# A fused S5 state-space and SwiGLU kernel: the first token block chunk by chunk through three features, its first weights in pieces of two features, and the parameter work behind all roots

## The chip, the cores and the metric

The kernel runs on one core of a Trainium2 chip. A core has a matrix engine (TensorE, written PE in the profile, with its weight loads in a row of their own, PEld), a vector engine (VectorE, DVE), an engine for activation functions (ScalarE, ACT), a general engine (GpSimd, POOL) and a queue that mostly starts transfers (SyncE, SP). The metric is the device time of one execution in microseconds. The kernel before takes 212.93 us, the median of three executions (212.89, 212.93, 213.28).

## The reference

The input x has 2048 tokens of 512 values (bf16). Every token is normalised, and three terms are added:

```python
xn = _layernorm(x, axis=-1)
# A: a diagonal complex recurrence over the tokens
Lam_bar = exp(exp(log_dt) * Lambda)
B_bar = ((Lam_bar - 1) / Lambda)[:, None] * Bmat
h_t = Lam_bar * h_(t-1) + B_bar @ xn_t
A = 2 * real(h @ Cmat.T) + xn * Dskip
# B: a gated feed-forward layer, 512 -> 1792 -> 512
B = (silu(xn @ w1) * (xn @ w3)) @ w2
out = x + A + B
```

The state has 512 complex entries. `Lambda_re`, `Lambda_im` and `log_dt` are the "parameters" below: 512 numbers each, from which the columns and tables of the recurrence are made once, at the start.

## The kernel before, in words

The tokens are cut into four blocks of 512, each block into four chunks of 128. The 1792 features of the feed-forward layer are 14 tiles of 128, called features 0 to 13 here. For each block the kernel runs three stages: `glu_up` (gate and up projections, L358), `ssm_in` (the input projection of the recurrence, L388) and `y_out` (the down projection and the state's output, L461). The order of the stages is glu_up 0, ssm_in 0, ssm_in 1, glu_up 1, y_out 0, and so on to y_out 3.

The schedule is manual (L68): every engine executes its instructions in the order in which the program writes them, and the framework adds the waits. Work of VectorE that isn't urgent (statistics of later blocks, tables, the recurrence) stands in a queue of tasks, each with a cost in microseconds, and `drain` (L339) takes tasks from it at a given rate while the matmuls are written.

One matmul here has a stationary operand of 128x128 and streams up to 512 columns. For block 0 the stationary operands are pieces of w1 and w3 and the streamed columns are the normalised tokens, transposed (`xnT`), so `glu_mm` (L353) can process any stretch of tokens of a feature: four matmuls over the four parts of the inner dimension, for the columns `ts`.

What the change touches is the opening, before the first block runs at full width:

- L74 to L76: three small transfers of the parameters into `prm`, issued by ACT's queue. Then x of block 0, chunk by chunk, on SP's queue (L78, L79), then w1 and w3 by `load_w13` (L86): features 0 to 2, 3 to 5, x of block 1, features 6 to 9, 10 to 13.
- `keep_warm` (L133): matmuls of a zero tile into a bank that nobody reads. Five of 512 columns stand first (L138), three after the transpose of the parameters (L227, L228).
- `stats` (L146), `aggr` (L150), `rstd_act` (L153) and `normed` (L172): the normalisation of a chunk on DVE, ACT (Ln, then Exp) and DVE. `turn` (L231) transposes a normalised chunk on TensorE into PSUM, four transposes of 128x128, and `put` (L237) copies it into `xnT` on ACT or DVE.
- `par_cols` (L253): the parameters' columns, two activations on ACT and six small operations on POOL; `r_col` (L497) is an Exp of POOL's first product.
- L485 to L514: the order of all this. Parameter columns first; then chunks 0 and 1 up to `xnT`; then chunks 2 and 3 to `xn`, with a table load for Silu on ACT behind their roots (L503); then features 0 to 2 for the columns of chunks 0 and 1 (256 columns), with the transposes of chunks 2 and 3 put in ahead of the last group; then the two copies.

`glu_up(0, 1.3, begun)` (L524) takes the three begun features, adds the columns of chunks 2 and 3 and goes on with feature 3 at full width. [...]

Of the kernel before, what the change touches and what calls it, by code (L numbers as in the profile page):

```python
# [15 lines left out]
BF16 = DT.bfloat16  # L16
P = 128
# [3 lines left out]
def kernel(  # L21
# [24 lines left out]
    nc = tc.nc  # L46
# [3 lines left out]
    TBLK = 512  # L50
# [4 lines left out]
    NDT = D // P  # L55
    NPT = PS // P
# [7 lines left out]
    const = ctx.enter_context(tc.tile_pool(name="const", bufs=1))  # L64
    xpool = ctx.enter_context(tc.tile_pool(name="xpool", bufs=NBLK))
    work = ctx.enter_context(tc.tile_pool(name="work", bufs=2))
    psum = ctx.enter_context(tc.tile_pool(name="psum", bufs=8, space=bass.MemoryType.PSUM))
    ctx.enter_context(tc.manual_schedule())  # L68

    def ps_tile(name):  # L70
        return psum.tile([P, 512], FP32, name=name, tag="ps")


    prm = const.tile([3 * NPT, P], BF16, name="prm")  # L74
    for i, src in enumerate((A_Lambda_re, A_Lambda_im, A_log_dt)):
        nc.scalar.dma_start(out=prm[i * NPT:(i + 1) * NPT, :], in_=src.rearrange("(t p) -> t p", p=P))  # L76
    x_blk = [xpool.tile([P, CPB, D], BF16, name="x_blk") for _ in range(NBLK)]
    for c in range(CPB):  # L78
        nc.sync.dma_start(out=x_blk[0][:, c, :], in_=xv[:, 0, c, :])  # L79
    w1_sb = const.tile([P, NDT, F], BF16, name="w1_sb")  # L80
    w3_sb = const.tile([P, NDT, F], BF16, name="w3_sb")
    w2_sb = const.tile([P, NFT, D], BF16, name="w2_sb")
    w1v = B_w1.rearrange("(t p) f -> p t f", p=P)
    w3v = B_w3.rearrange("(t p) f -> p t f", p=P)

    def load_w13(f0, f1):  # L86
        fs = slice(f0 * P, f1 * P)
        nc.sync.dma_start(out=w1_sb[:, :, fs], in_=w1v[:, :, fs])
        nc.sync.dma_start(out=w3_sb[:, :, fs], in_=w3v[:, :, fs])

    dskip_row = const.tile([P, D], BF16, name="dskip_row")
# [3 lines left out]
    def load_turned(dst, src):  # L95
        for t in range(NDT):
            nc.sync.dma_start_transpose(out=dst[:, t, :], in_=src[:, t * P:(t + 1) * P])

    load_w13(0, 3)
    load_w13(3, 6)  # L100
    nc.sync.dma_start(out=x_blk[1], in_=xv[:, 1, :, :])
    load_w13(6, 10)
    load_w13(10, NFT)
    nc.sync.dma_start(out=dskip_row, in_=A_Dskip.partition_broadcast(P))
# [8 lines left out]
        load_turned(ct[1], A_C_im)  # L113


    warm = const.tile([P, 512], BF16, name="warm")
    nc.vector.memset(warm, 0.0)
    halfpi = const.tile([P, 1], FP32, name="halfpi")
    nc.vector.memset(halfpi, float(np.pi / 2))
# [2 lines left out]
    ident = const.tile([P, P], BF16, name="ident")  # L122
# [8 lines left out]
    wps = ps_tile("warm_ps")  # L131

    def keep_warm(n, width=512):  # L133
        for _ in range(n):
            nc.tensor.matmul(out=wps[:, :width], lhsT=warm[:, :P], rhs=warm[:, :width], start=True, stop=True)  # L135

    nc.scalar.preload_act_table_set("natural_log_exp_and_others")
    keep_warm(5)  # L138


    mv_all = const.tile([P, NBLK * CPB, 2], FP32, name="mv_all")
    rstd_all = const.tile([P, NBLK * CPB], FP32, name="rstd_all")
    xnTs = [None] * NBLK
    sums = {}

    def stats(c):  # L146
        sums[c] = work.tile([P, 6], FP32, name="stats", bufs=4)
        nc.vector.bn_stats(out=sums[c], in_=x_blk[c // CPB][:, c % CPB, :])  # L148

    def aggr(c):  # L150
        nc.vector.bn_aggr(out=mv_all[:, c, :], in_=sums.pop(c))

    def rstd_act(c0, c1):  # L153
        y = rstd_all[:, c0:c1]
        nc.scalar.activation(out=y, in_=mv_all[:, c0:c1, 1], func=ACT.Ln, bias=eps)
        nc.scalar.activation(out=y, in_=y, func=ACT.Exp, scale=-0.5)
# [15 lines left out]
    def normed(c):  # L172
        xn = work.tile([P, D], BF16, name="xn", bufs=8)
        nc.vector.tensor_scalar(out=xn, in0=x_blk[c // CPB][:, c % CPB, :], scalar1=mv_all[:, c, 0:1],
                                scalar2=rstd_all[:, c:c + 1], op0=ALU.subtract, op1=ALU.mult)
        return xn
# [47 lines left out]

    new_xnT(0)
    pprm = psum.tile([P, 3 * NPT], BF16, name="prm_ps", tag="ps")
    nc.tensor.transpose(out=pprm, in_=prm, identity=ident[:3 * NPT, :3 * NPT])  # L227
    keep_warm(3)  # L228
    xn0 = xns_of[0] = {}

    def turn(c):  # L231
        pxt = psum.tile([P, NDT, P], BF16, name="xt_ps", tag="ps")
        for dt in range(NDT):
            nc.tensor.transpose(out=pxt[:, dt, :], in_=xn0[c][:, dt * P:(dt + 1) * P], identity=ident)  # L234
        return pxt

    def put(c, pxt, eng):  # L237
        dst = xnTs[0][:, :, c * P:(c + 1) * P]
        if eng is nc.scalar:
            nc.scalar.activation(out=dst, in_=pxt, func=ACT.Copy)  # L240
        else:
            nc.vector.tensor_copy(out=dst, in_=pxt)  # L242
# [10 lines left out]
    def par_cols():  # L253
        prmc = const.tile([P, 3 * NPT], FP32, name="prmc")
        nc.scalar.activation(out=prmc, in_=pprm, func=ACT.Copy)
        col["lre"], col["lim"], col["ldt"] = (prmc[:, i * NPT:(i + 1) * NPT] for i in range(3))
        nc.scalar.activation(out=c4("dt"), in_=col["ldt"], func=ACT.Exp)
        nc.gpsimd.tensor_tensor(out=c4("kr"), in0=col["dt"], in1=col["lre"], op=ALU.mult)
        nc.gpsimd.tensor_tensor(out=c4("ki"), in0=col["dt"], in1=col["lim"], op=ALU.mult)
        nc.gpsimd.tensor_scalar(out=c4("turn"), in0=col["ki"], scalar1=float(1.0 / (2.0 * np.pi)), scalar2=None,  # L260
                                op0=ALU.mult)
        tt = nc.gpsimd.tensor_tensor
        tt(out=c4("den"), in0=col["lre"], in1=col["lre"], op=ALU.mult)
        tt(out=c4("d2"), in0=col["lim"], in1=col["lim"], op=ALU.mult)
        tt(out=col["den"], in0=col["den"], in1=col["d2"], op=ALU.add)
# [73 lines left out]
    def drain(us):  # L339
        credit[0] = min(credit[0] + us, us + 1.5)  # L340
        while queue and credit[0] > 0:
            cost, task = queue.popleft()
            credit[0] -= cost
            task()
# [8 lines left out]
    def glu_mm(b, f, w_sb, ps, ts):  # L353
        for dt in range(NDT):
            nc.tensor.matmul(out=ps[:, ts], lhsT=w_sb[:, dt, f * P:(f + 1) * P], rhs=xnTs[b][:, dt, ts],  # L355
                             start=(dt == 0), stop=(dt == NDT - 1))

    def glu_up(b, rate, begun=()):  # L358
        hg[b] = work.tile([P, NFT, TBLK], BF16, name="hgT")
        late = None  # L360
        for f in range(NFT):
            if f < len(begun):
                g_ps, u_ps = begun[f]
                ts = slice(TBLK // 2, TBLK)
            else:
                g_ps, u_ps = ps_tile("g_ps"), ps_tile("u_ps")
                ts = slice(0, TBLK)
            glu_mm(b, f, w1_sb, g_ps, ts)
            glu_mm(b, f, w3_sb, u_ps, ts)
            sl16 = work.tile([P, TBLK], BF16, name="sl16", bufs=4)  # L370
            nc.scalar.activation(out=sl16, in_=g_ps, func=ACT.Silu)  # L371
            up16 = work.tile([P, TBLK], BF16, name="up16", bufs=4)
            nc.scalar.activation(out=up16, in_=u_ps, func=ACT.Copy)  # L373
            if for_act:
                for_act.popleft()()
            if late is not None:
                late()

            def late(f=f, sl16=sl16, up16=up16):
                nc.vector.tensor_tensor(out=hg[b][:, f, :], in0=sl16, in1=up16, op=ALU.mult)  # L380

            drain(rate)
        late()
# [98 lines left out]
                nc.sync.dma_start(out=ov[:, c, ds], in_=o16[:, ds])  # L482


    AHEAD = 3  # L485
    par_cols()
    for c in range(2):
        stats(c)
        aggr(c)
        rstd_act(c, c + 1)  # L490
    xn0[0] = normed(0)
    xn0[1] = normed(1)
    put(0, turn(0), nc.scalar)
    keep_warm(2, P)
    put(1, turn(1), nc.scalar)
    keep_warm(4, 2 * P)
    nc.scalar.activation(out=r_col, in_=col["kr"], func=ACT.Exp)  # L497
    stats(2)
    stats(3)
    aggr(2)  # L500
    aggr(3)
    rstd_act(2, 4)
    nc.scalar.preload_act_table_set("silu_and_others")  # L503
    xn0[2] = normed(2)
    xn0[3] = normed(3)
    begun = []
    for f in range(AHEAD):
        begun.append((ps_tile("g_ps"), ps_tile("u_ps")))
        glu_mm(0, f, w1_sb, begun[f][0], slice(0, TBLK // 2))
        if f == AHEAD - 1:  # L510
            t2, t3 = turn(2), turn(3)
        glu_mm(0, f, w3_sb, begun[f][1], slice(0, TBLK // 2))
    put(2, t2, nc.scalar)
    put(3, t3, nc.vector)  # L514

    push([(3.2, par_turns), (0.2, par_recip)])
    push([(0.0, lambda: for_act.extend(par_trig()))])
# [4 lines left out]
    push([(1.2, par_out)])  # L522
    push(ln_tasks(2))
    glu_up(0, 1.3, begun)  # L524
    assert not for_act
    ssm_in(0, 0.8)
# [3 lines left out]
    push(res_tasks(2))  # L530
    push(res_tasks(3))
    glu_up(1, 1.35)
    y_out(0, 4.0)
    ssm_in(2, 0.85)
    glu_up(2, 1.35)
    y_out(1, 4.0)
    ssm_in(3, 0.85)
# [33 lines left out]
```

## Time and profile before

| what | value |
|---|---|
| median of three executions | 212.93 us (212.89 to 213.28) |
| the profiled execution | 213.02 us |
| its span, first to last instruction | 211.2 us |
| PE busy | 207.1 us, 98% of the span |
| DVE busy | 173.3 us, 82% |
| ACT busy | 94.0 us, 45% |
| POOL busy | 5.4 us, 3% |
| first useful matmul (L355) | starts at 7.12 us |
| feature 3 of block 0 (L355, 512 columns) | starts at 13.17 us |

The span is measured from the first instruction to the last; the execution's own time is 1.82 us longer. Times in the timeline are microseconds from the start of the span. A line of it gives the start, the duration, the engine, the line of the program, the operation, output and inputs by the program's names, the shape, and how many such instructions were merged into the line; in brackets stands how long the engine had been idle and what ended it. Matmuls overlap one another, so the distance between two starts says what one costs, and not the duration of one. PEclk, the clock that the throttle granted, is full in every slice.

### The profile page before, as it was taken

The page shows a single profiled execution, that of the slowest core. Times are in us where ns is not written, and L with a number is a line of the kernel's source. Part 1 is how long each engine was busy: PE and PEld are TensorE (multiplying, and loading weights), DVE is VectorE, ACT ScalarE, POOL GpSimd, SP SyncE. Part 2 cuts the span into 40 slices and gives each one's busy share as a digit, 9 for nine tenths or more (in the row PEclk, how much of TensorE's full clock was granted, in tenths as well). Part 3 has the DMA queues.
Part 4 walks back from the last instruction along what each step waited for, and adds up shares of the span by engine and source line. Part 5 has one row for each costly group of instructions (what it writes and reads, how often), then busy time and mean ns, then how long its engine had stood idle before and what let it go on. Part 6 is the DMA issues. An engine that isn't in the chain of part 4 may idle for free.

```text
span 211.2 us, 2809 instructions
## 1 busy us (share of the span) xinstructions
PE 207.1 (98%) x1005; PEld 97.3 (46%) x1005; DVE 173.3 (82%) x343; ACT 94.0 (45%) x164; POOL 5.4 (3%) x27
## 2 busy tenths in 40 slices
PE   7999999999999999999999999999999999999994
PEld 2764444444444444444444444444444444444453
DVE  4599899997999999999999999999999999121111
ACT  4689866666666300066666600036666630000000
POOL 4000230000000000000000000000000000000000
PEclk9999999999999999999999999999999999999999
DMA  5999589953000000000002100100000000000010
GB/s 151 342 348 199 93 191 327 221 124 75 0 0 3 0 25 25 25 26 3 0 0 67 33 3 25 50 25 0 5 0 0 0 0 26 28 25 25 33 44 26
DMA packets 26054, 13.69 MB, mean 65 GB/s; under 512 B 15928, under 2 KB 26040, under 8 KB 26040
## 3 DMA queue, kind: packets, MB, share of 16 engines
q1 hardware_dynamic: 26016, 13.51, 26.3%
q8 instruction: 8, 0.13, 0.3%
q14 instruction: 6, 0.05, 0.1%
q10 hardware_dynamic: 24, 0.00, 0.0%
HBM read 7.74 MB, written 2.10 MB: 47 GB/s over the span
## 4 chain that ended last, share of the span: by engine, by line
PE 97%; DMA 1%; ACTq 0%; DVE 0%; issue 0%
PE g_ps L355 23%; PE y_ps L471 23%; PE u_ps L355 23%; PE y_ps L476 13%; PE bu_ps L394 13%; PE warm_ps L135 1%; DMA prm<-in_A_log_dt_dram 1%; PE xt_ps L234 1%; ACTq L76 0%; DVE xnT L242 0%; DVE o L481 0%; PE prm_ps L227 0%
## 5 line engine op out<-in xcount | busy, mean ns | idle before, releaser
L355 PEld LDWEIGHTS <-w_sb 128*128 128x128 bf16 x472 | 46.0, 98 | 51.0 <-DVE xnT L242 0.4
L355 PE MATMUL g_ps<-xnT,w_sb 128*128 128x512 bf16 (+1 forms) x236 | 58.0, 368 | 0.1
L355 PE MATMUL u_ps<-xnT,w_sb 128*128 128x512 bf16 (+1 forms) x236 | 58.0, 368 | 0.0
L471 PE MATMUL y_ps<-w_sb,hgT 128*128 128x512 bf16 (+2 forms) x238 | 51.2, 366 | 0.0
L373 ACT ACTIVATE up<-u_ps 128x512 bf16<-128x512 f32 x56 | 33.5, 598 | 15.8 <-PE u_ps L355 15.3
L396 ACT ACTIVATE u<-bu_ps 128x512 bf16<-128x512 f32 x32 | 19.1, 597 | 46.3 <-PE bu_ps L394 46.3
L371 ACT ACTIVATE sl<-g_ps 128x512 bf16<-128x512 f32 x56 | 33.4, 597 | 10.6 <-PE g_ps L355 10.4
L428 DVE TENSOR_TENSOR_SCAN ab<-r_col,h,ab 128x256 bf16<-128x256 f32 x56 | 37.6, 731 | 0.2
L471 PEld LDWEIGHTS <-hgT 128*128 128x128 bf16 x238 | 22.8, 98 | 25.9
L481 DVE TENSOR_TENSOR o<-y_ps,x_blk 128x512 bf16<-128x512 f32 (+2 forms) x17 | 11.1, 653 | 24.3 <-PE y_ps L476 24.3
L476 PE MATMUL y_ps<-ct,h 128*128 128x512 bf16 (+2 forms) x136 | 30.4, 366 | 0.0
L394 PE MATMUL bu_ps<-xnT,bt 128*128 128x512 bf16 x128 | 28.1, 379 | 0.0
L380 DVE TENSOR_TENSOR hgT<-sl,up 128x512 bf16<-128x512 bf16 x56 | 23.0, 414 | 3.1 <-ACT up L373 3.1
L476 PEld LDWEIGHTS <-h 128*128 128x128 bf16 x136 | 13.0, 98 | 14.7
L394 PEld LDWEIGHTS <-bt 128*128 128x128 bf16 x128 | 12.5, 98 | 15.1
L148 DVE BATCH_NORM_STATS2 stats<-x_blk 128x6 f32<-128x512 bf16 x16 | 10.5, 675 | 1.7 <-DMA x_blk<-in_A_x_dram 1.7
L437 DVE TENSOR_TENSOR ab<-ab,tab_s 128x2048 bf16<-128x2048 bf16 x8 | 9.8, 1223 | 0.2
L433 DVE TENSOR_TENSOR ab<-ab,tab_c 128x2048 bf16<-128x2048 bf16 x8 | 9.8, 1221 | 0.1
L413 DVE TENSOR_TENSOR ab<-u,tab_y 128x2048 bf16<-128x2048 bf16 x8 | 9.7, 1218 | 0.0
L410 DVE TENSOR_TENSOR ab<-u,tab_x 128x2048 bf16<-128x2048 bf16 x8 | 9.7, 1217 | 0.0
L183 DVE TENSOR_TENSOR x_blk<-xd,x_blk 128x512 bf16<-128x512 bf16 x16 | 6.8, 428 | 0.5
L182 DVE TENSOR_TENSOR xd<-xn,dskip_row 128x512 bf16<-128x512 bf16 x16 | 6.7, 418 | 0.0
(72 smaller groups left out, 80.0 us busy)
## 6 DMA issues: line engine op xcount, KB each, us to landing
w_sb<-in_B_w_dram SPq DMA_DIRECT2D x4, 512.0 KB, 8.2
out_dram<-o SPq DMA_DIRECT2D x15, 128.0 KB, 1.7
w_sb<-in_B_w_dram SPq DMA_DIRECT2D x1, 1792.0 KB, 8.1
w_sb<-in_B_w_dram SPq DMA_DIRECT2D x4, 384.0 KB, 4.4
x_blk<-in_A_x_dram SPq DMA_DIRECT2D x3, 512.0 KB, 6.8
x_blk<-in_A_x_dram SPq DMA_DIRECT2D x4, 128.0 KB, 2.3
xnT<-xn SPq DMA_TRANSPOSE x12, 2.4
dskip_row<-in_A_Dskip_dram SPq DMA_DIRECT2D x1, 128.0 KB
```

The costliest lines, as they stand in the source:

```text
L148: nc.vector.bn_stats(out=sums[c], in_=x_blk[c // CPB][:, c % CPB, :])
L355: nc.tensor.matmul(out=ps[:, ts], lhsT=w_sb[:, dt, f * P:(f + 1) * P], rhs=xnTs[b][:, dt, ts], start=(dt == 0), stop=(dt == NDT - 1))
L371: nc.scalar.activation(out=sl16, in_=g_ps, func=ACT.Silu)
L373: nc.scalar.activation(out=up16, in_=u_ps, func=ACT.Copy)
L380: nc.vector.tensor_tensor(out=hg[b][:, f, :], in0=sl16, in1=up16, op=ALU.mult)
L394: nc.tensor.matmul(out=u_ps, lhsT=bt[ri][:, dt, pt * P:(pt + 1) * P], rhs=xnTs[b][:, dt, :], start=(dt == 0), stop=(dt == NDT - 1))
L396: nc.scalar.activation(out=u16[:, :, pt, ri, :], in_=u_ps.rearrange("p (s t) -> p s t", s=NSB), func=ACT.Copy)
L428: nc.vector.tensor_tensor_scan(out=a[:, pt, 2 * ri + 1, :], data0=r_b, data1=a[:, pt, 2 * ri, :], initial=init, op0=ALU.mult, op1=ALU.add)
L433: nc.vector.tensor_tensor(out=a[:, :, 0::2, :], in0=a[:, :, 1::2, :], in1=tab_b("c"), op=ALU.mult)
L471: nc.tensor.matmul(out=y_ps[:, ds], lhsT=hg[b][:, f, cl * P:(cl + 1) * P], rhs=w2_sb[:, f, ds], start=(f == 0), stop=False)
L476: nc.tensor.matmul(out=y_ps[:, ds], lhsT=h_tiles[i][:, pt, ri, h_ts], rhs=ct[ri][:, pt, ds], start=False, stop=(pt == NPT - 1 and ri == 1))
L481: nc.vector.tensor_tensor(out=o16[:, ds], in0=y_ps[:, ds], in1=x_blk[b][:, cl, ds], op=ALU.add)
```

## The change

It changes the order and the grain of the opening; nothing after feature 2 of block 0 is written differently.

- ACT's queue begins with the first table load, then issues w1 of features 0 and 1, and then the three parameter transfers. `load_w13` gets an argument for the queue of its first half. The weights of features 0 to 5 come in three pairs of pieces of two features, not two pairs of three.
- The warm-up tile is 128 columns wide instead of 512 and is read repeatedly by a broadcast; eight warm-ups of 512 columns stand first, four of 128 columns behind the transposes of chunk 0, and the others are gone.
- The transposes and copies of chunk 0 are cut into two halves with a PSUM tile each: ACT copies one, DVE the other. `turn` and `put` get a range.
- Every chunk has its own root (`rstd_act` of one column). Statistics, roots, normalisations and copies of neighbouring chunks are interleaved on DVE and ACT.
- Features 0 and 1 run chunk by chunk (128 columns) for chunks 0, 1 and 2, feature 2 for chunks 0 and 1 together (256 columns) and then chunk 2. `glu_up` adds chunk 3 alone.
- The transpose of the parameters, their columns, `r_col` and the table load for Silu come behind the fourth root. The copy of chunk 3 is on ACT behind them.

```diff
-    prm = const.tile([3 * NPT, P], BF16, name="prm")
-    for i, src in enumerate((A_Lambda_re, A_Lambda_im, A_log_dt)):
-        nc.scalar.dma_start(out=prm[i * NPT:(i + 1) * NPT, :], in_=src.rearrange("(t p) -> t p", p=P))
...
-    def load_w13(f0, f1):
+    def load_w13(f0, f1, first=nc.sync):
         fs = slice(f0 * P, f1 * P)
-        nc.sync.dma_start(out=w1_sb[:, :, fs], in_=w1v[:, :, fs])
+        first.dma_start(out=w1_sb[:, :, fs], in_=w1v[:, :, fs])
         nc.sync.dma_start(out=w3_sb[:, :, fs], in_=w3v[:, :, fs])
...
-    load_w13(0, 3)
-    load_w13(3, 6)
+    nc.scalar.preload_act_table_set("natural_log_exp_and_others")
+    load_w13(0, 2, nc.scalar)
+    prm = const.tile([3 * NPT, P], BF16, name="prm")
+    for i, src in enumerate((A_Lambda_re, A_Lambda_im, A_log_dt)):
+        nc.scalar.dma_start(out=prm[i * NPT:(i + 1) * NPT, :], in_=src.rearrange("(t p) -> t p", p=P))
+    load_w13(2, 4)
+    load_w13(4, 6)
...
-    warm = const.tile([P, 512], BF16, name="warm")
+    warm = const.tile([P, P], BF16, name="warm")
...
     def keep_warm(n, width=512):
+        rhs = warm.unsqueeze(1).to_broadcast([P, width // P, P])
         for _ in range(n):
-            nc.tensor.matmul(out=wps[:, :width], lhsT=warm[:, :P], rhs=warm[:, :width], start=True, stop=True)
-
-    nc.scalar.preload_act_table_set("natural_log_exp_and_others")
-    keep_warm(5)
+            nc.tensor.matmul(out=wps[:, :width], lhsT=warm, rhs=rhs, start=True, stop=True)
+
+    keep_warm(8)
...
     pprm = psum.tile([P, 3 * NPT], BF16, name="prm_ps", tag="ps")
-    nc.tensor.transpose(out=pprm, in_=prm, identity=ident[:3 * NPT, :3 * NPT])
-    keep_warm(3)
...
-                ts = slice(TBLK // 2, TBLK)
+                ts = slice(TBLK - P, TBLK)
...
-    AHEAD = 3
+    def new_xt(n=NDT):
+        return psum.tile([P, n, P], BF16, name="xt_ps", tag="ps")
+
+    def ahead(fs, w_sbs, c0, c1):
+        for f in fs:
+            for w_sb in w_sbs:
+                glu_mm(0, f, w_sb, begun[f][w_sb is w3_sb], slice(c0 * P, c1 * P))
+
+    H = NDT // 2
+    ta, tb, t1 = new_xt(H), new_xt(H), new_xt()
+    begun = [(ps_tile("g_ps"), ps_tile("u_ps")) for f in range(3)]
+
+    stats(0)
+    aggr(0)
+    rstd_act(0, 1)
+    stats(1)
+    xn0[0] = normed(0)
+    aggr(1)
+    rstd_act(1, 2)
+    turn(0, ta, 0, H)
+    turn(0, tb, H, NDT)
+    keep_warm(4, P)
+    put(0, ta, nc.scalar, 0, H)
+    stats(2)
+    put(0, tb, nc.vector, H, NDT)
+    xn0[1] = normed(1)
+    aggr(2)
+    rstd_act(2, 3)
+    stats(3)
+    ahead((0, 1), (w1_sb,), 0, 1)
+    turn(1, t1)
+    put(1, t1, nc.vector)
+    ahead((0, 1), (w3_sb,), 0, 1)
+    nc.tensor.transpose(out=pprm, in_=prm, identity=ident[:3 * NPT, :3 * NPT])
+    xn0[2] = normed(2)
+    aggr(3)
+    rstd_act(3, 4)
     par_cols()
-    for c in range(2):
-        stats(c)
-        aggr(c)
-        rstd_act(c, c + 1)
-    xn0[0] = normed(0)
-    xn0[1] = normed(1)
-    put(0, turn(0), nc.scalar)
-    keep_warm(2, P)
-    put(1, turn(1), nc.scalar)
-    keep_warm(4, 2 * P)
     nc.scalar.activation(out=r_col, in_=col["kr"], func=ACT.Exp)
-    stats(2)
-    stats(3)
-    aggr(2)
-    aggr(3)
-    rstd_act(2, 4)
     nc.scalar.preload_act_table_set("silu_and_others")
-    xn0[2] = normed(2)
     xn0[3] = normed(3)
-    begun = []
-    for f in range(AHEAD):
-        begun.append((ps_tile("g_ps"), ps_tile("u_ps")))
-        glu_mm(0, f, w1_sb, begun[f][0], slice(0, TBLK // 2))
-        if f == AHEAD - 1:
-            t2, t3 = turn(2), turn(3)
-        glu_mm(0, f, w3_sb, begun[f][1], slice(0, TBLK // 2))
-    put(2, t2, nc.scalar)
-    put(3, t3, nc.vector)
+    ahead((0, 1), (w1_sb, w3_sb), 1, 2)
+    ahead((2,), (w1_sb,), 0, 2)
+    t2, t3 = new_xt(), new_xt()
+    turn(2, t2)
+    put(2, t2, nc.vector)
+    ahead((2,), (w3_sb,), 0, 2)
+    ahead((0,), (w1_sb, w3_sb), 2, 3)
+    turn(3, t3)
+    put(3, t3, nc.scalar)
+    ahead((1, 2), (w1_sb, w3_sb), 2, 3)
```

More of the change, by code (lines that the diff above doesn't have):

```diff
@@ L226, with turn, put @@
     pprm = psum.tile([P, 3 * NPT], BF16, name="prm_ps", tag="ps")
-    nc.tensor.transpose(out=pprm, in_=prm, identity=ident[:3 * NPT, :3 * NPT])
-    keep_warm(3)
     xn0 = xns_of[0] = {}
[L231 to L238, printed above, removed]
+    def turn(c, pxt, d0=0, d1=NDT):
+        for dt in range(d0, d1):
+            nc.tensor.transpose(out=pxt[:, dt - d0, :], in_=xn0[c][:, dt * P:(dt + 1) * P], identity=ident)
+    def put(c, pxt, eng, d0=0, d1=NDT):
+        dst = xnTs[0][:, d0:d1, c * P:(c + 1) * P]
         if eng is nc.scalar:
```

## The prediction

> **What bounds the kernel now.** I read the page first: the busy shares and the chain that ended last.
>
> ```profile
> PE 207.1 (98%) x1005; PEld 97.3 (46%) x1005; DVE 173.3 (82%) x343; ACT 94.0 (45%) x164; POOL 5.4 (3%) x27
> PE 97%; DMA 1%; ACTq 0%; DVE 0%; issue 0%
> ```
>
> TensorE (PE) is busy for 98% of the span and is 97% of the chain. So only two things shorten the kernel: fewer matmul cycles, or useful matmuls that start earlier. The change takes no useful matmul away, so the opening decides. I read it in the timeline of the first 14 us (start, duration, instruction).
>
> ```profile
> 1.17 2.31 PE L135 MATMUL warm_ps<-warm 128*128 128x512 bf16 x5 [1.17 <-DVE eps L121]
> 2.79 0.69 DVE L148 BATCH_NORM_STATS2 stats<-x_blk 128x6 f32<-128x512 bf16 x1 [1.66 <-DMA x_blk<-in_A_x_dram]
> 3.51 0.18 DVE L151 BATCH_NORM_AGGREGATE mv_all<-stats 128x2 f32<-128x6 f32 x1
> 3.84 0.18 ACT L255 ACTIVATE prmc<-prm_ps 128x12 f32<-128x12 bf16 x1 [0.62 <-PE prm_ps L227]
> 4.05 0.21 ACT L257 ACTIVATE c_dt<-prmc 128x4 f32<-128x4 f32 x1
> 4.16 0.28 ACT L155 ACTIVATE rstd_all<-mv_all,eps 128x1 f32<-128x1 f32 x1
> 4.47 0.20 ACT L156 ACTIVATE rstd_all<-rstd_all 128x1 f32<-128x1 f32 x1
> 4.71 0.83 DVE L174 TENSOR_SCALAR xn<-x_blk,mv_all,rstd_all 128x512 bf16<-128x512 bf16 x2 [0.22 <-ACT rstd_all L156]
> 5.18 0.61 PE L234 MATMUL xt_ps<-ident,xn 128*128 128x128 bf16 x4
> 5.83 1.24 ACT L240 ACTIVATE xnT<-xt_ps 128x512 bf16<-128x512 bf16 x2 [0.73 <-PE xt_ps L234]
> 6.22 1.05 PE L135 MATMUL warm_ps<-warm 128*128 128x256 bf16 x4
> 7.12 0.60 PE L355 MATMUL g_ps<-xnT,w_sb 128*128 128x256 bf16 x4
> 7.65 0.61 PE L355 MATMUL u_ps<-xnT,w_sb 128*128 128x256 bf16 x4
> 9.41 0.61 PE L234 MATMUL xt_ps<-ident,xn 128*128 128x128 bf16 x8
> 9.85 0.60 PE L355 MATMUL u_ps<-xnT,w_sb 128*128 128x256 bf16 x4
> 10.54 0.61 PE L355 MATMUL g_ps<-xnT,w_sb 128*128 128x256 bf16 x4
> 13.17 1.03 PE L355 MATMUL g_ps<-xnT,w_sb 128*128 128x512 bf16 x4
> ```
>
> Four readings. The first useful matmul starts at 7.12, behind a chain: x lands, statistics, root, normalise, transpose, copy out. Feature 3, the first at full width, starts at 13.17 (call this T3); from there to 211.2 are 198.03 us that the change leaves alone. So the forecast is the shift of T3. Third, the four warm-up matmuls of 256 columns from 6.22 take until about 7.07, 213 ns each, while useful ones of 256 columns take 0.435 us for four, 109 ns: TensorE runs at half rate until about 6.95, some 5.8 us after its first matmul, although the granted clock is 1.00 throughout. Fourth, PE waits little after 7.12: 0.21 for weights before 7.65, 0.36 for a transposed chunk before 10.54.
>
> **The change, part by part.** The sum is made against the profiled execution: 213.02 us, span 211.2, so 1.82 around it. It lies 0.09 above the median of 212.93.
>
> Parameter work leaves the front. ACT's prmc and c_dt (3.84, 4.05) no longer precede the first Ln. The first aggregation ends at 3.69, so Ln starts at 3.74, Exp 0.31 later (4.16 to 4.47), normalisation 0.24 after that (4.47 to 4.71): 4.29. The second statistics, ahead of it on DVE, run 3.61 to 4.27, so 4.30, 0.41 earlier. Turning chunk 0 starts 0.47 later (4.71 to 5.18): 4.77. This needs ACT free at 3.74. The table load (1.28) goes first, from 0.71 to 1.99, then four issues: one of weights (SP's early ones take 0.43 to 0.51) and three of prm (0.56, 0.26, 0.31), to about 3.6 if nothing overlaps. Margin 0.1; if the queue runs beside the load, 1.4.
>
> Warm-ups. The three after the prm transpose, the two of 128 and the four of 256 columns go; they filled waits and cost nothing. DVE's memset of 512 columns takes 0.27; a quarter of it lets PE start at about 1.0. Eight matmuls at 0.43 run to 4.43. PE then idles 0.34 until 4.77; before, it idled 0.37 from 3.27 to 3.64.
>
> Chunk 0 is copied out in halves. At half rate two transposes are ready 0.44 after the start (four took 0.65, two cost 0.21): 5.21. ACT first does the second root (aggregation 4.63 to 4.81, Ln 4.86, Exp 5.17), so its half starts at 5.28. 256 columns take between 0.20 (the tiny ACT forms) and 0.60 (512 columns); I take 0.40: 5.68. DVE does the third statistics first (4.80 to 5.48), then its half, between 0.21 and 0.42, taken 0.27: 5.75. So one chunk is ready at 5.80 where two were ready at 7.07.
>
> Work of features 0 to 2. Before: 48 matmuls of 256 columns at 109 ns, 5.2 us. After: 8 of 256 and 80 of 128. The last 22 matmuls of the kernel are also 128 columns wide with new weights each; the chain of waits has them as
>
> ```profile
> 207.27 0.78 PE y_ps L471 x14
> 208.05 0.46 PE y_ps L476 x8
> ```
>
> that is 56 ns each. So 80 × 56 + 8 × 109 = 5.35 us: +0.13. [...] The trace here has 56.
>
> Now the order, with full rate from 6.95 as in the trace. Chunk 0 against w1, 8 matmuls at 107 ns: 5.80 to 6.65. Chunk 1 was normalised by DVE at about 5.75 to 6.15; its turn runs 6.65 to 7.02 and is copied out 7.25 to 7.67 (0.42), DVE having finished aggregation and statistics at 6.9. Chunk 0 against w3: to 7.46, then the prm transpose. Chunk 1, 16 matmuls: 7.72 to 8.60. Feature 2 w1, 4 of 256: 9.04. Turn 2: 9.26. Feature 2 w3: 9.70. Copy 2 is out at 9.95 (9.53 + 0.42), a wait of 0.3. Feature 0 chunk 2: 10.0 to 10.44; turn 3: 10.66; features 1 and 2 chunk 2: 11.54. Copy 3 on ACT is queued behind the parameter columns, the POOL product and the table load. The third and fourth normalisations follow at 7.6 and 8.68, the fourth root's Exp at 8.44, so prmc 8.55, c_dt 8.75, r_col 0.55 later (c_dt to POOL's product took 0.5): 9.3, table load 9.5 to 10.8, copy 3 10.9 to 11.5. It ends with the matmuls. Chunk 3, 24 matmuls: 11.55 to 12.87. T3 is 12.87: −0.30.
>
> If full rate comes by 5.8, chunk 1 goes out at 6.85 to 7.27 and everything follows 0.4 earlier: T3 = 12.47, −0.70. If it comes at 7.85: 13.07, −0.10. The four times shown (212.89, 212.93, 213.02 profiled, 213.28) are as they would be if the moment wanders a little. Eight full warm-ups fill 1.0 to 4.43 without the gap at 3.27, so I lean to the earlier half: −0.50.
>
> Weights. w1 of features 0 and 1 is 262 KB instead of 393, issued by ACT between 0.75 and 2.0 instead of SP's 2.64. Summing the half-microsecond rows of DMA rates, x and the first 393 KB (917 KB) were moved by 5.65; the new w1 is inside 786 KB, moved by about 5.3; the old piece was moved by 5.65 and landed at 6.24 (2.64 + 3.6), so the new one lands near 5.8, just in time, or earlier. w3, inside 1.05 MB: moved by 6.1, about 6.8 landed, needed at 7.0. SP gets one issue more (0.5) ahead of block 1's x and all later loads; those are used from 14.2 on, and the transposed B at 32: no cost. The three prm transfers, now behind w1 on ACT's queue, are issued by 3.6 and land 1.9 later (1.59 to 3.50 in the chain before): 5.5, and PE asks for them at 7.46: no cost unless they are 2 us late, when every later matmul would wait behind that transpose. POOL's c_turn ends near 10.0 and DVE's next work needs it only at 10.0 to 10.4, where it started at 10.39: nothing. ACT starts evacuating at 11.9 instead of 11.18 against an earlier T3; each feature takes it 1.2 to 1.85 and PE 1.73, and the banks of feature 0 are needed again at T3 + 1.73 = 14.6, freed at 13.1: nothing.
>
> **Rivals.** (a) The clock does not come. The new PE idles (0.34 at 4.43, some 0.15 at 5.63) restart whatever releases the full rate. 5.8 us after 4.77 is 10.6; until then chunk 0 w3 ends at 7.93, chunk 1 takes 1.70 (to 9.73), feature 2 w1 0.85 (10.58), and the rest at full rate gives T3 = 14.42: +1.25, 214.3. For it: a third of the opening is transposes and idling. Against: the 0.37 gap before did no such harm. Each microsecond of delay costs about 0.5, and it decides from about 8.1 on. [...]
>
> (b) Transfers collide. If ACT issues w1 at 0.75, its 262 KB share the engines with chunks x 1 to 3. Ahead of x 2 wholly it costs 262 KB at 263 GB/s (the row at 2.5 to 3.0), 1.0 us; not at all, 0. x 2 was due at 3.7 to 4.3 and its statistics, which stand ahead of the chunk 0 copy on DVE, need it at 4.80, so 0 to 0.5 late: T3 between 12.67 and 13.35, so 212.5 to 213.2.
>
> (c) Weight loads bind. If loads of 98 ns did not overlap, 80 × (98 − 56) = +3.4, 216. The tail speaks against it.
>
> (d) PE hardly waits at all: 5.80 + 5.35 + 16 transposes less 4 (0.67) gives 11.9: −1.2, 211.8.
>
> **How the numbers follow.** About 0.2% (0.43 us) is what a measurement can tell from no change. Forecast (0.56): −0.10 to −0.70, taken −0.50 from 212.93, 212.43; 0.40 of it beyond 0.43. (b) 0.18: 0.04 faster, 0.12 same, 0.02 slower. (a) 0.17, nearly all slower. (c) 0.02. (d) 0.07. Together faster 0.51, same 0.28, slower 0.21. The range reaches (a) at 214.3 and part of (d), 211.9; left out are (c), a later (a) and the best of (d), some 0.15. The forecast's own is 212.2 to 212.85.
>
> **What would show it.** First Ln at 3.74 and first normalisation at 4.30; first useful matmul near 5.8; 128-column matmuls 56 ns apart; the step from 107 to 56 ns by 7; waits of 0.3 or less before chunks 2 and 3; feature 3 at 12.5 to 12.9, and 198.0 us from there. I am wrong if the first statistics start after 2.8, if the table load ends after copy 3 is turned, or if 107 ns lasts past 8.

## The result, and the profile after

The changed kernel takes 214.50 us (median of 22 executions, 213.06 to 214.94); the kernel before, on the same chips, 213.08 (22 executions, 212.85 to 213.93). The ratio is 1.0053, with a 95% interval of 1.0038 to 1.0068 (the two medians alone would give 1.0067): slower, where a gain of 0.50 us was forecast. The times lie in two groups: 17 between 214.19 and 214.94, and 5 between 213.06 and 213.37. The profiled execution took 214.55, its span is 212.8; it belongs to the larger group.

The page, busy times and chain:

```profile
PE 206.6 (97%) x1025; PEld 98.8 (46%) x1043; DVE 173.6 (82%) x345; ACT 93.5 (44%) x165; POOL 5.5 (3%) x27
PE 94%; DMA 2%; ACT 1%; issue 1%; DVE 1%; SPq 0%; ACTq 0%
```

TensorE still bounds the kernel, but 2% of the chain is now a transfer, and the page's chain by line names it: x. The timeline of the opening (start, duration, instruction):

```profile
0.71 1.28 ACT L96 ACT_TABLE_LOAD   x1 [0.71 <-PEq L574]
0.74 0.45 ACTq L85 DMA_DIRECT2D w_sb<-in_B_w_dram  x1
0.97 3.60 PE L138 MATMUL warm_ps<-warm 128*128 128x512 bf16 x8 [0.97 <-DVE eps L123]
1.22 0.65 ACTq L100 DMA_DIRECT2D prm<-in_A_Lambda_re_dram  x1
1.91 0.26 ACTq L100 DMA_DIRECT2D prm<-in_A_Lambda_im_dram  x1
3.15 0.69 DVE L150 BATCH_NORM_STATS2 stats<-x_blk 128x6 f32<-128x512 bf16 x1 [2.23 <-DMA x_blk<-in_A_x_dram]
4.54 0.25 ACTq L100 DMA_DIRECT2D prm<-in_A_log_dt_dram  x1
4.54 0.69 DVE L150 BATCH_NORM_STATS2 stats<-x_blk 128x6 f32<-128x512 bf16 x1 [0.47 <-DMA x_blk<-in_A_x_dram]
4.84 0.29 ACT L157 ACTIVATE rstd_all<-mv_all,eps 128x1 f32<-128x1 f32 x1 [2.84 <-DMA x_blk<-in_A_x_dram]
5.40 0.41 DVE L176 TENSOR_SCALAR xn<-x_blk,mv_all,rstd_all 128x512 bf16<-128x512 bf16 x1 [0.17 <-ACT rstd_all L158]
5.87 0.61 PE L233 MATMUL xt_ps<-ident,xn 128*128 128x128 bf16 x4 [1.31 <-DVE xn L176]
6.79 1.01 PE L353 MATMUL g_ps<-xnT,w_sb 128*128 128x128 bf16 x8
7.60 0.63 PE L233 MATMUL xt_ps<-ident,xn 128*128 128x128 bf16 x4
8.02 1.06 PE L353 MATMUL u_ps<-xnT,w_sb 128*128 128x128 bf16 x8
9.54 0.47 PE L353 MATMUL u_ps<-xnT,w_sb 128*128 128x128 bf16 x4
9.85 0.39 PE L353 MATMUL g_ps<-xnT,w_sb 128*128 128x128 bf16 x4
10.07 0.39 PE L353 MATMUL u_ps<-xnT,w_sb 128*128 128x128 bf16 x4
14.54 1.03 PE L353 MATMUL g_ps<-xnT,w_sb 128*128 128x512 bf16 x3
```

Four things are to be seen.

- **x is late.** The first statistics start at 3.15 (2.79 before), the second at 4.54 (3.61 before), each after a wait that an x transfer ends. w1 was issued at 0.74, two hundredths of a microsecond after the first chunk of x.
- **ACT stands still for 2.84 us**, and what ends it is an x transfer, although ACT reads no x. Between the second and the third parameter issue its queue pauses from 2.17 to 4.54. The third issue comes at 4.54, in the moment in which the second statistics have their chunk (4.28 and 4.29 in the run with eleven warm-ups below). That it waits for x chunk 1 is read from these times; why it has to was not shown. The first Ln stands behind it: 4.84 instead of 4.11, when the first aggregation was ready (3.88 + 0.18 and 0.05).
- **TensorE idles 1.31 us** ahead of the first transposes. The profile counts from the modelled end of the last warm-up; in the measure of the prediction, start of the last warm-up (3.93) plus 0.43, it is 1.5, where 0.34 was forecast.
- **Full rate comes at 9.71.** Eight matmuls of 128 columns from 6.79 to the next transposes at 7.60 cost 0.81, some 100 ns each and so half rate; four from 9.54 cost 0.31, four from 9.85 cost 0.22, 56 ns each. The packed trace has the moment as a record of its own: the full clock is granted from 9.71 on. In the kernel before it is granted from 7.14 on, 0.2 later than the 6.95 that the prediction took from the spacing. PEclk shows 1.00 ahead of these moments too, because the record only begins there and a stretch without a record counts as full.

Feature 3 starts at 14.54 instead of 13.17. This shift of 1.37 carries to the end: the last copy to the output starts at 209.90 instead of 208.53. The remaining 0.2 of the two spans lies behind that copy: from feature 3 to the end are 198.24 us here and 198.07 before. The traces below fall into the same two groups, 198.03 to 198.08 (the kernel before, also with the gap, and the three runs with all parameters on POOL) and 198.23 to 198.27 (all others). The cause is open.

So three causes stood to be told apart: x made late by w1, ACT blocked by the third parameter issue, and the half rate that lasts longer after idling; and beside them the finer grain and the new order themselves.

### The profile page after: what moved, and what is told of

Its sections match the earlier page's. It is cut to its first block, busy times and chain, and to the rows that moved or that the text cites. A ratio compares the mean times of both kernels' runs of the same rounds, so it can differ in the third digit from the quotient of the medians.

```text
span 212.8 us, 2874 instructions
## 1 busy us (share of the span) xinstructions
PE 206.6 (97%) x1025; PEld 98.8 (46%) x1043; DVE 173.6 (82%) x345; ACT 93.5 (44%) x165; POOL 5.5 (3%) x27
## 4 chain that ended last, share of the span: by engine, by line
PE 94%; DMA 2%; ACT 1%; issue 1%; DVE 1%; SPq 0%; ACTq 0%
PE u_ps L353 23%; PE y_ps L469 23%; PE g_ps L353 22%; PE y_ps L474 13%; PE bu_ps L392 13%; DMA x_blk<-in_A_x_dram 2%; ACT up L371 1%; PE xt_ps L233 1%; DVE xnT L240 0%; PE warm_ps L138 0%; DVE xn L176 0%; SPq L76 0%; ACT rstd_all L157 0%; DVE o L479 0%; ACTq L100 0%
## 5 line engine op out<-in xcount | busy, mean ns | idle before, releaser
L353 PEld LDWEIGHTS <-w_sb 128*128 128x128 bf16 x512 | 47.8, 100 | 50.2 <-issue 0.3
L353 PE MATMUL u_ps<-xnT,w_sb 128*128 128x512 bf16 (+2 forms) x255 | 59.2, 356 | 0.3
L353 PE MATMUL g_ps<-xnT,w_sb 128*128 128x512 bf16 (+2 forms) x249 | 58.3, 356 | 0.3
L392 PEld LDWEIGHTS <-bt 128*128 128x128 bf16 x128 | 12.5, 98 | 15.1
L150 DVE BATCH_NORM_STATS2 stats<-x_blk 128x6 f32<-128x512 bf16 x16 | 10.6, 673 | 2.7 <-DMA x_blk<-in_A_x_dram 2.7
```

The source lines that it names most:

```text
L392: nc.tensor.matmul(out=u_ps, lhsT=bt[ri][:, dt, pt * P:(pt + 1) * P], rhs=xnTs[b][:, dt, :], start=(dt == 0), stop=(dt == NDT - 1))
```

## The experiments

Each kernel differs from the changed kernel by the edit shown, unless another is named as its start. Ratios are to the kernel before, timed beside it (medians 213.18 beside the first four, 213.29 beside the next four, 213.06 beside the last).

**Parameters on POOL.** This takes the block off ACT and leaves the transfers as they are.

```diff
-        nc.scalar.dma_start(out=prm[i * NPT:(i + 1) * NPT, :], ...)   # behind w1
+        nc.gpsimd.dma_start(out=prm[i * NPT:(i + 1) * NPT, :], ...)   # behind iota_f
```

> The changed kernel with its three parameter transfers issued by POOL instead of ACT; nothing else differs. In the changed kernel's trace ACT issues the third of them at 4.54, the moment in which x chunk 1 lands, and the first Ln behind it starts at 4.84, although the first aggregation ended at 4.06. Theory 'ACT is blocked': with nothing queued ahead, Ln starts at 4.11 and the first normalisation follows; feature 3 starts well over 0.5 us earlier than 14.54 and the kernel takes 213.9 or less. Theory 'x is late': the first normalisation still stands behind the second statistics on DVE, which wait for x chunk 1 (landed 4.54, done 5.23), so it moves from 5.40 to 5.23 only and the kernel gains 0.1 to 0.3 us: about 214.3.

212.92, ratio 0.9998 (0.9984 to 1.0013). The time is what the first theory allowed (213.9 or less), but neither had the size: the step was 1.6 us. Its timeline:

```profile
3.88 0.29 ACT L157 ACTIVATE rstd_all<-mv_all,eps 128x1 f32<-128x1 f32 x1 [1.88 <-DVE mv_all L153]
4.33 0.69 DVE L150 BATCH_NORM_STATS2 stats<-x_blk 128x6 f32<-128x512 bf16 x1 [0.49 <-DMA x_blk<-in_A_x_dram]
4.94 0.40 DVE L176 TENSOR_SCALAR xn<-x_blk,mv_all,rstd_all 128x512 bf16<-128x512 bf16 x1
5.40 0.61 PE L233 MATMUL xt_ps<-ident,xn 128*128 128x128 bf16 x4 [0.83 <-DVE xn L176]
8.66 0.49 PE L353 MATMUL g_ps<-xnT,w_sb 128*128 128x128 bf16 x4
8.99 0.39 PE L353 MATMUL u_ps<-xnT,w_sb 128*128 128x128 bf16 x4
9.22 0.39 PE L353 MATMUL g_ps<-xnT,w_sb 128*128 128x128 bf16 x4
```

Ln is free at 3.88, and the first normalisation now waits for the second statistics, which wait for x, as the second theory had it. The first transposes moved by 0.47 only, and 0.21 of it is that x chunk 1 landed earlier in this execution (4.33 for 4.54). But the idling shrank to 0.83, and of twelve executions nine lie between 212.72 and 213.10, three at 213.72 to 213.89. The profiled one is of the three: its full rate comes at 8.90 (four matmuls cost 0.33 from 8.66, 0.23 from 8.99) and feature 3 at 13.90. So a fair part of the gain isn't in the chain of dependences at all.

**w1 back on SP.**

```diff
-    load_w13(0, 2, nc.scalar)
+    load_w13(0, 2)
```

> The changed kernel with w1 of features 0 and 1 issued by SP behind x, as all other weights, and not by ACT. Theory 'x is late because w1's 262 KB share the transfer engines with it': the first statistics start at about 2.8 (3.15 in the changed kernel), the second at 3.6 (4.54), the first normalisation at 4.3 (5.40), TensorE idles 0.35 us instead of 1.3 in front of the first transposes, full rate comes by about 7, and feature 3 starts at 12.9 (14.54): about 212.7, 0.1 to 0.2% under the kernel before. Rival 'the grain of 128 columns, or the order on DVE and ACT, costs the time': x is early, but feature 3 still starts at 13.5 or later and the kernel stays above 213.5. Third possibility: the weights come too late from SP (w1 needed at 5.8, before that it landed at 6.24 with 393 KB): a wait of up to 0.5 us before the first useful matmul, about 213.0.

212.83, ratio 0.9987 (0.9969 to 1.0004); eleven executions between 212.43 and 213.33, one at 214.51.

```profile
2.91 0.69 DVE L150 BATCH_NORM_STATS2 stats<-x_blk 128x6 f32<-128x512 bf16 x1 [1.98 <-DMA x_blk<-in_A_x_dram]
3.74 0.66 DVE L150 BATCH_NORM_STATS2 stats<-x_blk 128x6 f32<-128x512 bf16 x1
4.42 0.41 DVE L176 TENSOR_SCALAR xn<-x_blk,mv_all,rstd_all 128x512 bf16<-128x512 bf16 x1
5.81 0.61 PE L353 MATMUL g_ps<-xnT,w_sb 128*128 128x128 bf16 x8 [0.30 <-ACT xnT L238]
7.38 0.62 PE L353 MATMUL u_ps<-xnT,w_sb 128*128 128x128 bf16 x8 [0.75 <-DMA w_sb<-in_B_w_dram]
```

x is as early as before: the second statistics wait for nothing at 3.74, where they waited until 4.54. That w1 beside x made x late is thereby shown. ACT isn't blocked either (its three issues start at 0.74, 1.31 and 1.60), so this run takes the late x and the block away together. First normalisation and first useful matmul are where the prediction had them (4.30 and 5.80; here 4.42 and 5.81). What comes next is like the third possibility of the expectation, weights that come too late from SP, but it is w3 and not w1: TensorE waits 0.75 for w3 of features 0 and 1, and feature 3 starts at 13.19 in this execution, 213.22.

**Eleven warm-ups.** This fills the idling and leaves block and late x alone.

```diff
-    keep_warm(8)
+    keep_warm(11)
```

> The changed kernel with eleven warm-ups of 512 columns instead of eight; at 0.43 us each they end near 5.66, just ahead of the first transposes at 5.87, and fill the idle 1.3 us. x is as late as in the changed kernel. Theory 'idling holds the full rate back': matmuls of 128 columns step from 107 to 56 ns near 7 instead of near 9.6, and feature 3 starts at about 13.4 instead of 14.54: about 213.4, and the times scatter less. Rival 'the rate comes when it comes, whatever stood before': no change, 214.5.

213.15, ratio 1.0000 (0.9991 to 1.0009); all twelve executions lie between 213.03 and 213.45.

```profile
4.59 0.29 ACT L157 ACTIVATE rstd_all<-mv_all,eps 128x1 f32<-128x1 f32 x1 [2.59 <-DMA x_blk<-in_A_x_dram]
5.62 0.40 PE L233 MATMUL xt_ps<-ident,xn 128*128 128x128 bf16 x4 [0.41 <-DVE xn L176]
5.85 0.39 PE L138 MATMUL warm_ps<-warm 128*128 128x128 bf16 x4
13.11 1.03 PE L353 MATMUL g_ps<-xnT,w_sb 128*128 128x512 bf16 x4
```

ACT is blocked as before (2.59) and x is late (4.29), yet the whole loss is gone: feature 3 starts 1.43 earlier than in the changed kernel, and only 0.25 of that is x chunk 1, which landed earlier in this execution (4.29 for 4.54). The four transposes take 0.23 from start to start, 57 ns each; the full clock is granted from 4.43 on, even earlier than the 7 expected. At 4.43 eight warm-ups would only just have ended, so this one trace doesn't show what the three more did. The times do: none of the twelve lies above 213.45, where 17 of 22 lay above 214. Three matmuls of zeros are worth 0.5%.

**The kernel before, with a gap.** The counter-test on the old order, which has neither late x nor a block.

```diff
     nc.tensor.transpose(out=pprm, in_=prm, identity=ident[:3 * NPT, :3 * NPT])
-    keep_warm(3)
```

> The kernel before without the three warm-ups of 512 columns behind the parameters' transpose; TensorE then idles from about 3.8 to 5.2, 1.4 us. No computation is left out. Theory 'idling holds the full rate back': it comes some 3.8 us after the idling ends, as in the changed kernel (idle until 5.87, full rate near 9.6), so near 9.0 instead of 6.95; the useful matmuls from 7.12 to 9.0 run at half rate, so about +0.9 us: 213.9. Rival 'idling of this length does no harm': 213.0, as before.

213.92, ratio 1.0040 (1.0025 to 1.0055), times from 213.25 to 214.64.

```profile
5.18 0.61 PE L233 MATMUL xt_ps<-ident,xn 128*128 128x128 bf16 x4 [1.38 <-DVE xn L174]
7.11 0.94 PE L354 MATMUL g_ps<-xnT,w_sb 128*128 128x256 bf16 x4
7.89 0.60 PE L354 MATMUL u_ps<-xnT,w_sb 128*128 128x256 bf16 x4
8.33 0.60 PE L354 MATMUL g_ps<-xnT,w_sb 128*128 128x256 bf16 x4
```

The transposes start at 5.18 and the first useful matmul at 7.11, as before; but the first four cost 0.78, where the next four cost 0.44. In this execution, the fastest of the twelve, full rate comes at 7.84; the median is where the expectation had it, but the later full rate that the longer times point to was not traced. Idling alone makes the old kernel nearly as much slower as the change did (1.0040 and 1.0053, with intervals that overlap).

**Block and idling both gone** (parameters on POOL, and)

```diff
-    keep_warm(8)
+    keep_warm(10)
```

> The changed kernel with the parameter transfers on POOL and ten warm-ups of 512 columns, so that neither ACT's queue is blocked nor TensorE idles long. Against the run with eleven warm-ups alone (213.15, feature 3 at 13.11, first Ln at 4.59 behind the blocked issue) this prices the block without the clock. Theory 'the block itself costs the 0.2 to 0.3 us by which the first transposes move (5.62 to 5.40), and all the rest of its cost is the clock': feature 3 at 12.85 to 12.9, 212.9, with a scatter as small as with eleven warm-ups (0.4 us). Rival 'the block is covered once the clock is right': 213.15.

213.11, ratio 0.9995 (0.9986 to 1.0004). The rival holds: with the clock on time the block costs nothing that can be measured. The chain of this run, and its waits, say why:

```profile
2.58 4.64 DMA w_sb<-in_B_w_dram
```

```profile
PEld L353 <- DMA w_sb<-in_B_w_dram: 0.3, 1, 0.3
```

The first transposes moved forward, but the matmuls against w3 can't start before w3 has landed, at 7.22; feature 3 starts at 13.07, against 13.11 with the block.

**w1 on SP and nine warm-ups** (as the second experiment, and `keep_warm(9)`).

> The changed kernel with w1 of features 0 and 1 on SP and nine warm-ups, which end at 4.81 at the latest, beside the first transposes at 4.89: no idling over 0.3 us. This prices the new order and grain with x as early as before and with the full rate on time. Theory 'what then ends the opening are the weights': w3 of features 0 and 1, issued at 3.1, lands at 7.0 to 7.4 and TensorE waits 0.3 to 0.75 for it; feature 3 at 12.8 to 13.2, 212.6 to 212.9, without the run of 214.5 that eight warm-ups had. Rival 'grain and order cost': 213.1 or more.

213.03, ratio 0.9996 (0.9980 to 1.0012), with one execution at 214.82, where the expectation had none; it was not traced, and its cause is open. TensorE waits longer still for w3:

```profile
7.45 0.62 PE L353 MATMUL u_ps<-xnT,w_sb 128*128 128x128 bf16 x8 [0.88 <-DMA w_sb<-in_B_w_dram]
```

Feature 3 starts at 13.25. The time lies between the expected 212.6 to 212.9 and the rival's 213.1; the trace puts it on the weights (0.88 where 0.3 to 0.75 was expected) and not on the grain.

**The first normalisation ahead of the second statistics** (parameters on POOL, nine warm-ups, and)

```diff
-    stats(1)
     xn0[0] = normed(0)
+    stats(1)
```

> As with the parameters on POOL, with nine warm-ups, and with the first normalisation written ahead of the second statistics on DVE, so that chunk 0 no longer waits for x chunk 1. Theory 'chunk 0 is held by x chunk 1 only through DVE's order': the first normalisation starts at 4.45 instead of 4.94, the first useful matmul at 5.9 instead of 6.3; chunk 1 comes 0.1 later. Since the later chunks then set the end, feature 3 moves by 0 to 0.3: 212.65 to 212.9. Rival 'the wait moves to the next chunk in full': 213.0 or more.

213.10, ratio 0.9994 (0.9985 to 1.0002). The rival holds.

```profile
4.62 0.41 DVE L176 TENSOR_SCALAR xn<-x_blk,mv_all,rstd_all 128x512 bf16<-128x512 bf16 x1 [0.60 <-ACT rstd_all L158]
5.89 0.29 ACT L157 ACTIVATE rstd_all<-mv_all,eps 128x1 f32<-128x1 f32 x1 [1.30 <-DVE mv_all L153]
6.33 0.37 ACT L238 ACTIVATE xnT<-xt_ps 128x256 bf16<-128x256 bf16 x1
6.75 0.61 PE L353 MATMUL g_ps<-xnT,w_sb 128*128 128x128 bf16 x8 [1.03 <-ACT xnT L238]
```

Chunk 0 is normalised earlier, but its copy on ACT stands behind the second root, which waits for chunk 1's aggregation. The wait moved from one engine's order into another's: the first useful matmul starts at 6.75, where 5.9 was expected, and feature 3 at 13.62 in this execution, the slowest of the eleven (213.46).

**w1 behind two parameter transfers** (the third parameter transfer on POOL, nine warm-ups).

```diff
-    load_w13(0, 2, nc.scalar)
-    for i, src in ...: nc.scalar.dma_start(out=prm[...], ...)
+    load_prm(0, A_Lambda_re, nc.scalar)
+    load_prm(1, A_Lambda_im, nc.scalar)
+    load_w13(0, 2, nc.scalar)
...
+    load_prm(2, A_log_dt, nc.gpsimd)
-    keep_warm(8)
+    keep_warm(9)
```

(`load_prm` issues one of the three transfers on the queue that it is given.)

> The changed kernel with two of the parameter transfers ahead of w1 on ACT's queue (w1 is then issued near 1.6 instead of 0.74, when x has a lead), the third on POOL, and nine warm-ups instead of eight. Theory 'w1 issued beside x makes x late, and idling then holds the full rate back': x chunk 0 is there at 2.8 to 2.9, chunk 1 at 3.7 to 4.0 instead of 4.54, the first normalisation ends the second statistics' wait near 4.6 and feature 3 starts at 12.7: about 212.6, below the kernel before. Rival 'w1 delays x wherever it is issued from ACT': chunk 1 lands at 4.3 or later as with the parameters on POOL alone, about 212.9.

212.80 beside 213.29, ratio 0.9975 (0.9966 to 0.9984): the version that beats both kernels.

```profile
1.61 0.44 ACTq L85 DMA_DIRECT2D w_sb<-in_B_w_dram  x1
3.75 0.66 DVE L155 BATCH_NORM_STATS2 stats<-x_blk 128x6 f32<-128x512 bf16 x1
4.43 0.41 DVE L181 TENSOR_SCALAR xn<-x_blk,mv_all,rstd_all 128x512 bf16<-128x512 bf16 x1
5.40 0.69 DVE L155 BATCH_NORM_STATS2 stats<-x_blk 128x6 f32<-128x512 bf16 x1 [0.47 <-DMA x_blk<-in_A_x_dram]
6.34 0.50 PE L358 MATMUL g_ps<-xnT,w_sb 128*128 128x128 bf16 x6 [0.18 <-DVE xnT L245]
```

Chunks 0 and 1 of x come first, w1 second, and TensorE never waits for weights. Now chunk 2 is late (5.40), and the half copy of chunk 0 stands behind its statistics. Feature 3 starts at 12.84, 0.14 later than expected.

**The same, with the third statistics behind that copy and the second normalisation** on DVE.

> The run with w1 behind two parameter transfers, and on DVE the third statistics moved behind chunk 0's half copy and the second normalisation. In that run the third statistics waited for x chunk 2 until 5.40 and the half copy behind them ran at 6.01, so chunk 0 was complete at 6.30. Theory 'DVE's order holds chunk 0 behind x chunk 2': the copy runs at 5.4, the first eight matmuls at 5.8, and feature 3 starts 0.2 to 0.4 us earlier than 12.84: 212.4 to 212.6. Rival 'w3 of features 0 and 1, which lands near 7.0 to 7.2, ends the next wait': TensorE waits for it 0.3 to 0.6 us and feature 3 stays at 12.7 to 12.9: 212.7 to 212.8, no difference.

213.00 beside 213.06, ratio 0.9989 (0.9977 to 1.0001). The rival's number holds, its mechanism only in part. The copy runs at 5.45 instead of 6.01, but then both weights are waited for:

```profile
5.95 0.77 PEld L358 LDWEIGHTS <-w_sb 128*128 128x128 bf16 x8 [0.37 <-DMA w_sb<-in_B_w_dram]
5.95 1.04 PE L358 MATMUL g_ps<-xnT,w_sb 128*128 128x128 bf16 x8
7.23 0.45 PEld L358 LDWEIGHTS <-w_sb 128*128 128x128 bf16 x8 [0.16 <-DMA w_sb<-in_B_w_dram]
```

The first wait, the longer one, is for w1, whose transfer the run's chain has from 1.63 to 5.91; the second is for w3. Between them TensorE works at half rate (eight matmuls of 128 columns cost 0.83 from 5.95 to 6.78, 104 ns each), for the full clock is granted from 6.95 on only (5.99 in the run before this one), although TensorE hardly idles. Feature 3 starts at 13.04.

The idling and the times side by side (idling before the first transposes, start of the full clock and start of feature 3 from the profiled execution; medians of all):

| kernel | idle, us | full clock from | feature 3 | median, us |
|---|---|---|---|---|
| changed | 1.31 | 9.71 | 14.54 | 214.50 |
| parameters on POOL | 0.83 | 8.90 | 13.90 | 212.92 |
| w1 on SP | 0.63 | 3.81 | 13.19 | 212.83 |
| eleven warm-ups | 0.41 | 4.43 | 13.11 | 213.15 |
| before | none here (0.15 at 3.64) | 7.14 | 13.17 | 213.08 |
| before, with a gap | 1.38 | 7.84 | 13.40 | 213.92 |

With w1 on SP and with eleven warm-ups the full clock was there before the idling began.

## Why the prediction was wrong

**The forecast failed at its first step**, "Parameter work leaves the front", in the term that put Ln at 3.74 if ACT was free by 3.6. I added up the durations of four issues and asked only whether the queue runs beside the table load. It does (0.71 and 0.74). What I left out is that an issue can wait: the third one waited 2.37 us, until x chunk 1 was there, and Ln came at 4.84. What it cost stands in a later term: the sum had full rate from 6.95 or earlier, and it came at 9.71. With eleven warm-ups the block and the late x are still there, and feature 3 starts at 13.11. Two of the signs that the prediction names for being wrong came true: the first statistics start after 2.8 (3.15), and half rate lasts past 8.

**The step "Weights" failed with it.** I asked when w1 lands and, for the forecast, let x land as before. w1 issued beside x put the second statistics at 4.54, and x early again with w1 on SP shows that this was w1. Rival (b) had the mechanism at 0.18, but the wrong chunk: I followed x 2 to the third statistics and gave 0 to 0.5 us. It was x 1, whose statistics stand on DVE ahead of the first normalisation, a queue that I had written down in the step before. By 1.05 MB moved until 6.1 I had also put w3 at 6.8; where TensorE waited for it, it came between 7.2 and 7.8.

**Rival (a) is what happened, by another road.** Its price was T3 = 14.42 and 214.3; measured were 14.54 and 214.50. That the numbers lie so close is luck: the rival had the first useful matmul at 5.80 and full rate at 10.6, and they came at 6.79 and 9.71. I gave it 0.17 because the idling of 0.34 that I expected looked like the 0.37 before, which had done no harm. The traces with idling of 0.33 to 0.63 can't test that, since the full clock was granted in them before the idling began (3.81 to 4.43); but the idling was itself a result of the step that failed. 0.34 became 1.5 in the same measure (1.31 by the profile's) as soon as the first normalisation slipped from 4.30 to 5.40. I had treated (a) and (b) as separate cases with a chance each, while (b) sets off (a): a first normalisation 0.69 later than before (5.40 for 4.71) made a feature 3 that is 1.37 later.

**The gain that was forecast went to the transfers.** With the clock on time the changed kernel stands even with the one before (1.0000 with eleven warm-ups, 0.9995 with the block gone too) and not 0.2% below. Feature 3 then starts at 13.07 to 13.25 (13.62 with the first normalisation ahead), not at 12.5 to 12.9, because in none of these runs were x and the first w1 and w3 all there by 7: with w1 early x is late, with w1 on SP w3 is late. Only one run with the order x 0, x 1, w1 got 12.84. In the seven traces with full rate by 7, feature 3 starts 5.80 or 5.81 us after the first matmul against w3, so that matmul decides. The sum has nearly the same (7.02 to 12.87), but its T3 of 12.47 needs w3 at 6.6, earlier than the 6.8 of its own step on weights.

**What was right.** 128-column matmuls with new weights cost 56 ns (9.85, 10.07), so rival (c) does not hold here. The half copies took 0.37 and 0.29 (0.40 and 0.27 taken). The wait before chunk 2's matmuls was 0.23 (11.40 to 11.63); copy 3 on ACT, behind the table load, ran 12.50 to 13.10 while TensorE was busy; no wait of TensorE for a bank or for POOL's columns stands in the trace. From feature 3 to the last copy, nothing changed: 195.36 both times (209.90 − 14.54 and 208.53 − 13.17).

**What stays open.** That the five executions at 213.06 to 213.37 are those in which full rate came early is argued from eleven warm-ups giving 213.15; none of the five was traced. Nor do the runs show how much idling is borne: by the times, a kernel that idled 0.83 in its trace lost in three of twelve executions, one that idled 1.31 in 17 of 22. Single long times also occur where nothing idles long (214.82 with w1 on SP and nine warm-ups; 214.15 and 216.45 of the kernel before), and none of them was traced.

## What to carry to other kernels

Where TensorE starts at half rate, as here (some 100 ns for a matmul of 128 columns, 56 later), let filler matmuls reach to the first real work with margin: a first normalisation 0.7 us later cost twice that here, and three more matmuls of zeros took it back. A transfer moved to another engine's queue was not free of the old one here: look for what it now runs beside (w1 beside x: second statistics at 4.54 instead of 3.61), and whether an issue behind it has to wait for an earlier transfer (2.37 us, until x chunk 1 was there), with everything behind it on that engine. Give the first bytes needed the transfers to themselves; here the order chose which of x, w1 and w3 was late, and no order tried had all three in time.

## What the runs showed of the hardware that was not expected

The moment of full rate differed from trace to trace. By the clock records the full clock came at 3.81 in one trace, 2.85 us after the first warm-up (w1 on SP), and at 7.14 in another, 5.97 us after (before), with nearly the same warm-ups ahead of it; with w1 behind two parameter transfers it came at 5.99 and 6.95. After an idling of about 0.8 to 1.4 us it came 2.7 us (the old order with a gap), 3.5 us (parameters on POOL) and 3.8 us (changed) after work resumed. The times of these kernels spread over 1.2 to 1.9 us, against 0.36 to 0.84 in the five kernels that idled for 0.46 or less and had w1 on ACT; the two with w1 on SP spread over 2.1 us, by one execution each (214.51 and 214.82).

Once granted, the full clock stayed to the end of the span in both kernels: its record lasts 204.80 us in each, from 7.14 in a span of 211.2 (before) and from 9.71 in one of 212.8 (changed). What decides the moment of the grant was not shown.
